# Two query units in turn in the opening, a queue of values drained later, and later C loads, in a fused attention and state-space kernel

## The chip, the cores and the metric

The kernel runs on one core of a Trainium2 chip. The metric is device time in microseconds (us) of one execution. Executions of the same kernel scatter by some us here (967.45 to 972.73 us in eleven runs of the kernel before in one call), so timed runs are given as a median or mean with their number, and a profiled execution is one execution, not the typical one. The experiments were run in three calls on three chips (runs 1 to 4, 5 to 8 and 9 to 11, in the order below), and the kernel before took 970.06, 969.35 and 969.82 us in them (means): times of different calls are compared by what they save on the kernel before of the same call.

Ratios are the mean time of one kernel's fast runs over the mean of the other's from the same rounds, so they are not quite the ratios of the medians.

Engines: TensorE (PE in the profile; PEld is its weight load), VectorE (DVE), ScalarE (ACT), GpSimd (POOL), and SyncE (SP), which issues most DMAs (257 of the 264 in the profile of before).

## The reference, cut to what matters

```python
x = A_x                                            # 1 x 2048 x 1024, bf16
g = sigmoid((x * gate_w).sum(-1, keepdims=True))
a = ssm(x, Lambda, B, C, log_dt, Dskip)            # complex diagonal scan over 2048 steps, 1024 states
qkv = x @ wqkv                                     # 32 heads of 32
p = softmax(q @ k.T * 32 ** -0.5)                  # 2048 x 2048 for each head
b = (p @ v) @ wo
return g * a + (1 - g) * b
```

The softmax has 32 x 2048 x 2048 exponentials: 1,024 instructions of 128 x 1024 on ScalarE. Everything else is arranged around them.

## The kernel before

Eight groups of four heads; in each group eight query units of 256 queries; in each unit eight *bursts* of 256 keys, one for each x block. A burst is one score instruction group on TensorE and two exponentials on ScalarE. In the main loop, one burst is one *period*. In it TensorE does the scores of burst p, the values (exponentials times V) of burst p - 2, and four "dense" 512-column matmuls of other work (projections, B, C, output); VectorE evicts a dense chain from its PSUM bank when it ends, and does the scan's arithmetic.

```python
OPENING = ("K0 B0 K1 M B1 K2 Va0 B2 Vb0 Q1 Va1 K3 Vb1 B3 Va2 Vb2 K4 Va3 B4 Vb3 K5 Va4 B5 Vb4 K6 Va5 B6 Vb5 K7 Va6 B7 "
           "Vb6 Va7 Vb7 B8 P0 P1 P2 G B9 P3 P4 P5")     # Ki: keys of x block i; Bi: burst i; Va/Vb: values; P: p @ v

def burst(self, B):
    ...
    self.S.op("pe", mm, reads=[("K", g % 2, i // 2), ("Q", qz)], writes=[("S", sl[0]), ("S", sl[1])], name="qk")
    for z in range(2):
        s, p = sl[z], self.pt_of(B, z)
        self.act(lambda e, s=s, p=p: e.activation(self.tile[p], ps[:, 2 * s:2 * s + 2, :], ACT.Exp, scale=SCALE), [("S", s)], [("pt", p)], "exp")

def build(self):
    ...
    self.ld_b(0, 0)
    self.ld_b(1, 1)                  # B's first two blocks; two buffers in all
    for part in (1, 2, 0):
        self.ld_w(1, part)
    for j in range(8):
        self.ld_c(j)                 # 16 transposing loads of C, all here
    self.opening()
    ...
    for p in range(first, NBURST):   # first = 10
        self.burst(p)
        for b in pvs.get(p, [p - 2]):
            self.pv(b)               # the values of a burst: four quarters of four matmuls
        ...                          # then four dense matmuls, then VectorE's background work
        if ended is not None:
            ended.evac()             # VectorE empties bank 7; on a chain of B's block n this also issues the load of block n + 2
```

In SyncE's timeline the DMAs go out in the order of the program, and the load of B's third block is behind the 16 C loads (33.15 to 60.61 us): it goes out at 63.99 us here.

## Time and profile before

| | before |
|---|---|
| timed, three runs | 967.69, 969.53, 971.06 us |
| the profiled execution | 974.28 us (span 972.5 us) |
| ScalarE busy | 943.8 us |
| first exponential | 9.86 us |
| half-clock windows of TensorE (granted clock 0.50) | 66.7 us (6.8 us), 865.4 us (3.4 us), 957.5 us (6.8 us), 967.8 us on |

Busy time of each engine (share of the span) and the chain of waits, from the page of before:

```profile
PE 934.1 (96%) x15308; PEld 491.0 (50%) x15308; DVE 512.8 (53%) x1096; ACT 943.8 (97%) x1034; POOL 9.4 (1%) x39
...
ACT 94%; PE 3%; DVE 1%; DMA 1%; SPq 1%; issue 0%; DVEq 0%
```

ScalarE is busy 97% of the span and carries 94% of the chain that ended last. A change can only win from its idle time. The view of ScalarE's waits has them as: who waited, for whom, us in total, times, longest.

```profile
ACT f_pt L1530 <- PE f_ps L1524: 7.6, 6, 4.5
ACT f_OT L1530 <- PE f_ps L1524: 4.8, 3, 2.3
...
ACT f_Et L1530 <- PE f_ps L1524: 1.4, 2, 0.9
```

L1524 is the score matmul and L1530 the exponential: 13.8 us of ScalarE's idle time come from scores that were late. The timeline of ScalarE (start, duration, what, count, idle time before and its releaser) shows the opening's share:

```profile
14.68 1.94 ACT L1530 ACTIVATE f_pt<-f_ps 128x1024 bf16<-128x1024 f32 x2 [0.96 <-PE f_ps L1524]
18.95 1.94 ACT L1530 ACTIVATE f_OT<-f_ps 128x1024 bf16<-128x1024 f32 x2 [2.33 <-PE f_ps L1524]
22.60 1.94 ACT L1530 ACTIVATE f_OT<-f_ps 128x1024 bf16<-128x1024 f32 x2 [1.71 <-PE f_ps L1524]
...
25.37 1.94 ACT L1530 ACTIVATE f_OT<-f_ps 128x1024 bf16<-128x1024 f32 x2 [0.74 <-PE f_ps L1524]
27.81 1.94 ACT L1530 ACTIVATE f_Et<-f_ps 128x1024 bf16<-128x1024 f32 x2 [0.50 <-PE f_ps L1524]
30.67 3.78 ACT L1530 ACTIVATE f_Et<-f_ps 128x1024 bf16<-128x1024 f32 x4 [0.92 <-PE f_ps L1524]
```

Each line is one burst of two exponentials (the last is two bursts), and before each one ScalarE idles: one x block gives it 1.83 us of work, and the blocks come more slowly (from the fourth to the ninth, 7.61 to 20.55 us, the loads are issued 2.6 us apart). The second piece is later. SyncE's timeline, around the end of the C loads (L1052), two transposes of attention output (L1569) and the load of B's third block (L1046):

```profile
59.13 1.48 SPq L1052 DMA_TRANSPOSE f_cT_im<-in_A_C_im_dram  x1
60.73 3.17 SPq L1569 DMA_TRANSPOSE f_OT<-f_On  x2
63.99 1.27 SPq L1046 DMA_TRANSPOSE f_wb<-in_A_B_re_dram  x1
```

TensorE's timeline over the same time, with the dense matmuls of B at L1414, and its recovery:

```profile
63.34 0.57 PE L1546 MATMUL f_ps<-f_V,f_pt 128*128 128x33 bf16 x16
...
67.73 1.89 PE L1414 MATMUL f_ps<-f_xT,f_wb 128*128 128x512 bf16 x4 [3.82 <-DMA f_wb<-in_A_B_re_dram]
...
73.39 1.05 PE L1414 MATMUL f_ps<-f_xT,f_wb 128*128 128x512 bf16 x4
74.38 0.40 PE L1524 MATMUL f_ps<-f_Q,f_K 32*128 32x256 bf16 x8
...
76.08 0.40 PE L1524 MATMUL f_ps<-f_Q,f_K 32*128 32x256 bf16 x8
...
77.98 0.40 PE L1524 MATMUL f_ps<-f_Q,f_K 32*128 32x256 bf16 x8
```

TensorE stands 3.82 us for B's block. The first four matmuls after it take 1.89 us, where four take 1.05 us at 73.39: the clock was halved (granted clock 0.50 from 66.7 to 73.5 us). From 74 us TensorE is behind and runs as fast as it can (busy 12.86 of 13.00 us from 74 to 87 us): its period is 1.70 us (74.38 to 76.08) when a chain goes on, and 1.90 us (76.08 to 77.98) when a new one has to wait for the bank's eviction. ScalarE's period is 1.83 us, so TensorE has little room.

**An accounting used below.** From the start times in the trace: between the 301st and the 801st exponential, ScalarE starts one every 0.9167 us. How far the n-th exponential starts behind a ScalarE that kept this pace from the first one is called its *lag*. In the profile of before it is 7.9 us at the 33rd exponential (the opening), 7.8 at the 43rd, 13.4 at the 93rd (the stall), and stays there to the 901st.

Starts have a flaw here. Where exponentials follow one another without a delay, ScalarE's records grow from 1.02 to 1.33 us (in the profile of before from the 56th to the 82nd exponential): they start every 0.904 us, while they still end every 0.917. So a lag by starts comes out up to 0.31 us lower there than a lag by ends, and seems to fall although nothing was won. Where it matters, the lag by ends is given too.

### The profile page before, as it was taken

To read this page: it belongs to the slowest core of one execution; us is meant where nothing else is said; L and a number is where in the kernel's file an instruction comes from. 1 tells how busy PE (TensorE), PEld (TensorE's weight loads), DVE (VectorE), ACT (ScalarE), POOL (GpSimd) and SP (SyncE) were. 2 spreads that over 40 slices of the span, in tenths; PEclk is the share of its full clock that TensorE was granted. 3 is DMA by queue.
4 is the path that set the end of the run, shared out by engine and by line. 5 is a ranking of instruction groups with operands and counts; after the bars stand their busy time and mean duration, and the time that the engine had idled before them with its cause. 6 is when DMAs were issued, how large, how long until landed. Compare 5 with 4: busy or idle time off the path is not lost.

```text
span 972.5 us, 33344 instructions
## 1 busy us (share of the span) xinstructions
PE 934.1 (96%) x15308; PEld 491.0 (50%) x15308; DVE 512.8 (53%) x1096; ACT 943.8 (97%) x1034; POOL 9.4 (1%) x39
## 2 busy tenths in 40 slices
PE   7989999999999999999999999999999999899996
PEld 5534644464445464554644654545544556444443
DVE  3668889889888525412268611188744112232223
ACT  4979999999999999999999999999999999999996
POOL 1000000000000000000000000000000000000000
PEclk9989999999999999999999999999999999999997
DMA  9994014311232102120023110132101213223311
GB/s 203 154 170 85 8 29 80 73 30 37 40 72 61 49 5 51 39 69 29 19 37 83 30 37 28 50 82 62 29 5 51 83 37 105 57 74 115 114 60 61
DMA packets 157074, 60.88 MB, mean 63 GB/s; under 512 B 145664, under 2 KB 145664, under 8 KB 156928
## 3 DMA queue, kind: packets, MB, share of 16 engines
q1 hardware_dynamic: 154768, 58.16, 26.9%
q8 instruction: 121, 1.98, 0.9%
q10 hardware_dynamic: 2160, 0.53, 0.3%
q14 instruction: 25, 0.20, 0.1%
HBM read 16.79 MB, written 12.58 MB: 30 GB/s over the span
## 4 chain that ended last, share of the span: by engine, by line
ACT 94%; PE 3%; DVE 1%; DMA 1%; SPq 1%; issue 0%; DVEq 0%
ACT f_pt L1530 93%; SPq L1036 1%; PE f_ps L1524 1%; ACT f_OT L1530 1%; PE f_ps L1414 1%; DMA f_xT<-in_A_x_dram 1%; PE f_ps L1546 0%; PE f_ps L1153 0%; ACT f_Et L1530 0%; DMA f_wb<-in_A_B_re_dram 0%; PE f_ps L1474 0%; DVE f_V L1158 0%; PE f_ps L1117 0%; DVE f_K L1129 0%; PE f_ps L1754 0%
## 5 line engine op out<-in xcount | busy, mean ns | idle before, releaser
L1530 ACT ACTIVATE f_pt<-f_ps 128x1024 bf16<-128x1024 f32 x1006 | 923.3, 1310 | 7.6 <-PE f_ps L1524 7.6
L1546 PEld LDWEIGHTS f_ps<-f_V,f_pt 128*128 128x128 bf16 x8048 | 234.5, 96 | 106.9 <-issue 103.5
L1546 PE MATMUL f_ps<-f_V,f_pt 128*128 128x33 bf16 x8048 | 285.6, 178 | 0.0
L1524 PE MATMUL f_ps<-f_Q,f_K 32*128 32x256 bf16 x4096 | 204.6, 274 | 24.7 <-ACT f_pt L1530 6.5
L1524 PEld LDWEIGHTS f_ps<-f_Q,f_K 32*128 32x128 bf16 x4096 | 61.0, 92 | 229.7 <-ACT f_pt L1530 222.2
L1414 PE MATMUL f_ps<-f_xT,f_wb 128*128 128x512 bf16 x512 | 132.7, 381 | 4.0 <-DMA f_wb<-in_A_B_re_dram 3.8
L1384 PE MATMUL f_ps<-f_xT,f_wb 128*128 128x512 bf16 x472 | 121.0, 378 | 0.0
L1456 DVE TENSOR_SCALAR f_Ag<-f_ps,f_gcol 128x512 f32<-128x512 f32 x32 | 24.0, 751 | 135.4 <-PE f_ps L1443 135.4
L1333 DVE TENSOR_TENSOR_SCAN f_ht<-f_pf,f_init,f_ut 128x512 bf16<-128x512 f32 x64 | 80.4, 1273 | 0.0
L1443 PE MATMUL f_ps<-f_cT_re,f_hp 128*128 128x512 bf16 x192 | 72.7, 378 | 0.0
L1443 PE MATMUL f_ps<-f_cT_im,f_hp 128*128 128x512 bf16 x192 | 72.6, 378 | 0.0
L1474 PE MATMUL f_ps<-f_wb,f_OT 128*128 128x512 bf16 x252 | 67.4, 387 | 0.1
L1480 DVE SCALAR_TENSOR_TENSOR f_xT<-f_ps,f_gcol,f_hp 128x512 bf16<-128x512 f32 (+1 forms) x28 | 21.0, 751 | 77.2 <-PE f_ps L1474 77.2
L1402 PE MATMUL f_ps<-f_wb,f_xT 128*128 128x128 bf16 x896 | 59.3, 219 | 0.0
L1414 PEld LDWEIGHTS f_ps<-f_xT,f_wb 128*128 128x128 bf16 x512 | 40.7, 96 | 36.1 <-DMA f_wb<-in_A_B_re_dram 3.9
L1420 DVE CAST f_ub<-f_ps 128x512 bf16<-128x512 f32 x48 | 33.2, 692 | 46.8 <-PE f_ps L1414 46.4
L1384 PEld LDWEIGHTS f_ps<-f_xT,f_wb 128*128 128x128 bf16 x472 | 36.9, 96 | 28.1
L1402 PEld LDWEIGHTS f_ps<-f_wb,f_xT 128*128 128x128 bf16 x896 | 50.4, 97 | 0.0
L1391 DVE CAST f_Q<-f_ps 128x512 bf16<-128x512 f32 x31 | 21.5, 692 | 54.6 <-PE f_ps L1384 54.5
L1324 DVE TENSOR_TENSOR f_tq<-f_ht,f_Et 128x512 bf16<-128x512 bf16 x128 | 45.6, 419 | 0.0
L1324 DVE TENSOR_TENSOR f_ut<-f_tq 128x512 f32<-128x512 bf16 x64 | 42.0, 685 | 0.0
L1408 DVE CAST f_V<-f_ps 128x512 bf16<-128x512 f32 x28 | 19.4, 694 | 38.2 <-PE f_ps L1402 38.0
(124 smaller groups left out, 504.2 us busy)
## 6 DMA issues: line engine op xcount, KB each, us to landing
ag_scratch<-f_Ag SPq DMA_DIRECT2D x32, 256.0 KB, 2.0
f_hp<-ag_scratch SPq DMA_DIRECT2D x32, 256.0 KB, 2.9
f_wb<-in_B_wqkv_dram SPq DMA_DIRECT2D x21, 256.0 KB, 4.5
out_dram<-f_xT SPq DMA_DIRECT2D x16, 256.0 KB, 2.1
f_wb<-in_B_wo_dram SPq DMA_DIRECT2D x1, 1024.0 KB, 5.3
f_OT<-f_On SPq DMA_TRANSPOSE x63, 2.5
f_wb<-in_B_wo_dram SPq DMA_DIRECT2D x1, 768.0 KB
f_wb<-in_B_wqkv_dram ACTq DMA_DIRECT2D x2, 256.0 KB, 4.2
```

The lines of the kernel that those rows point to most:

```text
L1324: ops.append((c, lambda: dve(lambda e: e.tensor_tensor(o, a, b, op), r, w)))
L1333: ops.append((1.29, lambda ri=ri: dve(lambda e: e.tensor_tensor_scan(ht[:, ri, :], rr, ut[:, ri, :], self.init[:, ri, j:j + 1], ALU.mult, ...
L1384: mms.append((1, lambda e, f, l, a=a: e.matmul(ps[:, bank, :], w[:, g % 2, part, a, :], xT[:, a, 512 * ch:512 * (ch + 1)], start=f, stop=l ...
L1402: m = e.matmul(ps[:, bank, 128 * q:128 * (q + 1)], xT[:, a, 128 * kt:128 * (kt + 1)], w[:, g % 2, 2, a, :], start=(a == 0), stop=(a == 7))
L1414: mms.append((1, lambda e, f, l, a=a: e.matmul(ps[:, 7, :], bT[:, n % 2, ri, a, :], xT[:, a, 512 * ch:512 * (ch + 1)], start=f, stop=l), [ ...
L1420: self.dve(lambda e: e.tensor_copy(self.ub[k][:, ri, :], ps[:, 7, :]), [("bank", 7)], [("ub", k, ri)] + over, "evac_u")
L1443: mms.append((1, lambda e, f, l, j=j, ri=ri: e.matmul(ps[:, 7, :], hp[:, ri, j, cols], cT[ri][:, j, 512 * cb:512 * (cb + 1)], start=f, sto ...
L1456: self.dve(lambda e: e.tensor_scalar(a, ps[:, 7, :], self.gcol[:, 0, tt:tt + 1], None, ALU.mult), [("bank", 7), "g0"], [at], "evac_c")
L1474: mms.append((1, lambda e, f, l, j=j: e.matmul(ps[:, 7, :], OT[:, j, 256 * qb + 128 * r:256 * qb + 128 * (r + 1)], wo[j][0][:, 512 * cb:51 ...
L1524: m = e.matmul(ps[:, 2 * sl[h // 2] + h % 2, 256 * kl:256 * (kl + 1)], K[32 * h:32 * h + 32, g % 2, 128 * kt:128 * (kt + 1)], Q[32 * h:32 ...
L1530: self.act(lambda e, s=s, p=p: e.activation(self.tile[p], ps[:, 2 * s:2 * s + 2, :], ACT.Exp, scale=SCALE), [("S", s)], [("pt", p)], "exp")
L1546: m = e.matmul(ps[:, 6, o:o + 33], self.tile[p][:, h2, 256 * kl + 128 * qt:256 * kl + 128 * (qt + 1)], V[:, g % 2, 2 * i + kl, h, :], star ...
```

## The change

The intent: keep ScalarE fed while x lands, by taking two query units for each x block; let the exponentials of those 16 bursts wait in a queue of tiles, since no value matmuls are done in the opening; drain the queue with one or two quarters more in each period; and load C later, into space that the queue used first, so that B's loads are not behind it. The diff, cut to its core:

```diff
+FIRST = 16
+RING = 60
+C_LOADS = 28
...
-        pte = four(self.Et[:].rearrange("p r j t -> p (r j t)")[:, 0:6144])
-        self.tile = [self.pt[:, t] for t in range(6)] + [ptx[:, t] for t in range(6)] + [pte[:, t] for t in range(6)]
+        pte = four(self.Et[:].rearrange("p r j t -> p (r j t)"))
+        self.tile = [self.pt[:, t] for t in range(6)] + [ptx[:, t] for t in range(6)] + [pte[:, t] for t in range(8)]
+        self.tile += [self.cT[ri][:, j, :].rearrange("p (h n) -> p h n", h=2) for j in range(8) for ri in range(2)]
...
-    OPENING = ("K0 B0 K1 M B1 K2 Va0 B2 Vb0 Q1 Va1 K3 Vb1 B3 Va2 Vb2 K4 Va3 B4 Vb3 K5 Va4 B5 Vb4 K6 Va5 B6 Vb5 K7 Va6 B7 "
-               "Vb6 Va7 Vb7 B8 P0 P1 P2 G B9 P3 P4 P5")
+    OPENING = ("K0 B0.0 Ka1 Kb1 M B0.1 Qa1 Qb1 Va0 B1.0 Ka2 Kb2 B1.1 Vb0 Ka3 B0.2 Kb3 Va1 Ka4 B0.3 Kb4 Vb1 B0.4 Ka5 Kb5 B1.2 Va2 Ka6 "
+               "B0.5 Kb6 Vb2 Ka7 B0.6 Kb7 Va3 B0.7 Vb3 Qa2 Qb2 B1.3 Va4 Vb4 B1.4 Qa3 Qb3 Va5 B1.5 Vb5 B1.6 Va6 Vb6 B1.7 Va7 Vb7 G")
...
+        for p in range(FIRST, NBURST + 1):
+            n = min(4 * (p - 1), done + (12 if p < FIRST + 0 else 5), done // 32 * 32 + 32)
+            left = done // 32 * 32 + 32 - done
+            if 5 < left < 13 and 4 * (p - 1) >= done + 6:
+                n = done + 6
+            self.quarters[p] = (done, n)
... (each queued burst gets one of 18 pairs of tiles, for as long as its values are waited for)
-        for j in range(8):
-            self.ld_c(j)
+        self.plan()
         self.opening()
...
-        pvs = {10: [6, 7], 11: [8], 12: [9, 10]}
         for p in range(first, NBURST):
...
-            for b in pvs.get(p, [p - 2]):
-                self.pv(b)
+            q0, q1 = self.quarters[p]
+            self.pv(q0, q1)
...
+            if p >= C_LOADS and p % 4 == 0 and nc < 8:
+                self.ld_c(nc)
+                nc += 1
```

In `B1.2` the first number is the query unit, the second the x block; `Ka3` and `Kb3` are the halves of a key projection.

More of the change, by code (lines that the diff above doesn't have):

```diff
@@ L1052, in ld_c @@
             self.dma(lambda e, ri=ri, src=src: e.dma_start_transpose(self.cT[ri][:, j, :], src[:, 128 * j:128 * (j + 1)]),
-                     [], [("cT", ri, j)], "ld_cT")
+                     [], [("cT", ri, j), ("pt", 20 + 2 * j + ri)], "ld_cT")
     def begin(self):
@@ L1109, in piece, with half256 @@
             yield lambda mm=mm, kw=kw, r=r: self.S.op("pe", mm, reads=[("w", 0, part), ("xr", r)], name="proj", **kw)
-    def pieces256(self, part, i, bank):
+    def half256(self, part, i, half):
         ps, w, xT = self.ps, self.w, self.xT
@@ L1115, in mm @@
             m = None
-            for a in range(8):
-                m = e.matmul(ps[:, bank, 0:256], w[:, 0, part, a, :], xT[:, a, 256 * i:256 * (i + 1)], start=(a == 0), stop=(a == 7))
+            for a in range(4 * half, 4 * half + 4):
+                m = e.matmul(ps[:, 7, 0:256], w[:, 0, part, a, :], xT[:, a, 256 * i:256 * (i + 1)], start=(a == 0), stop=(a == 7))
             return m
-        self.S.op("pe", mm, reads=[("w", 0, part), ("xr", 2 * i), ("xr", 2 * i + 1)], writes=[("bank", bank)], name="proj")
+        self.S.op("pe", mm, reads=[("w", 0, part), ("xr", 2 * i), ("xr", 2 * i + 1)], name="proj", **(dict(acc=[("bank", 7)]) if half else dict(writes=[("bank", 7)])))
     def opening(self):
@@ L1132, in opening @@
         for word in self.OPENING.split():
-            op, i = word.rstrip("0123456789"), word.lstrip("KQVabPBMG")
-            i = int(i) if i else 0
+            op = word.rstrip("0123456789.")
+            i = word[len(op):]
+            U, i = [int(v) for v in i.split(".")] if "." in i else (0, int(i or 0))
             if op == "K":
-                if i == 0:
-                    for a, b in zip(self.piece(1, 0, 7, True), self.piece(0, 0, 6, True)):
-                        a()
-                        b()
-                    evac(self.Q[:, 0, 0:256], 6, ("Q", 0), True, self.act)
-                else:
-                    self.pieces256(1, i, 7)
+                for a, b in zip(self.piece(1, 0, 7, True), self.piece(0, 0, 6, True)):
+                    a()
+                    b()
+                evac(self.Q[:, 0, 0:256], 6, ("Q", 0), True, self.act)
+                evac(self.K[:, 0, 0:256], 7, ("K", 0, 0), True)
+            elif op in ("Ka", "Qa"):
+                self.half256(int(op == "Ka"), i, 0)
+            elif op == "Kb":
+                self.half256(1, i, 1)
                 evac(self.K[:, 0, 256 * i:256 * (i + 1)], 7, ("K", 0, i // 2), i % 2 == 0)
-            elif op == "Q":
-                self.pieces256(0, i, 7)
-                evac(self.Q[:, 0, 256 * i:256 * (i + 1)], 7, ("Q", 0), False)
+            elif op == "Qb":
+                self.half256(0, i, 1)
+                evac(self.Q[:, i // 2, 256 * (i % 2):256 * (i % 2 + 1)], 7, ("Q", i // 2), i % 2 == 0)
+                self.spare(0.5)
             elif op in ("Va", "Vb"):
-                bank, h, kt = 7 if i == 7 else 6, int(op == "Vb"), 2 * i + int(op == "Vb")
+                bank, h, kt = 6, int(op == "Vb"), 2 * i + int(op == "Vb")
                 def mm(e, kt=kt, h=h, bank=bank):
@@ L1160, in opening @@
                     dve(lambda e, i=i, src=src: e.tensor_copy(self.gcol[:, 0, 2 * i:2 * i + 2], src[:, :, 128]), [("bank", bank)], [("g0", i)])
-                    self.spare(0.9)
+                    self.spare(1.0)
             elif op == "G":
@@ L1167, in opening @@
                 dve(lambda e: e.tensor_scalar(g[:, 1, :], g[:, 0, :], -1.0, 1.0, ALU.mult, ALU.add), ["g0"], ["g1"])
-            elif op == "P":
-                if i == 0:
-                    S.tok_w["O"] = S.tok_w[("bank", 6)]
-                    S.tok_r["O"] = list(S.tok_r[("bank", 6)])
-                self.pv(i)
             elif op == "B":
-                self.p = i
-                self.burst(i)
-                while self.later and self.later[0][0] <= i:
+                self.burst(8 * U + i)
+                while self.later and self.later[0][0] <= self.p:
                     self.later.pop(0)[1]()
+                self.p += 1
             elif op == "M":
@@ L1300, in table_ops @@
         first = ["m_a0", "m_a1", "m_a2", "m_k", "m_h", "m_y", "m_s"] if j == 0 else []
-        over = [("pt", 12 + t) for t in range(6)] if j == 0 else []
+        over = [("pt", 12 + j // 2), ("pt", 16 + j // 2)]
         ops = []
@@ L1506, in st_out, with plan @@
                  [("fin", fb, 0), ("fin", fb, 1)], [("outd", tt)], "st_out")
+    def plan(self):
+        self.quarters, done = {}, 0
+        used = {}
+        for p in range(FIRST, NBURST + 1):
[4 more added lines that the diff above has]
+            self.quarters[p] = (done, n)
+            for q in range(done, n):
+                used[q // 4] = p
+            done = n
+        order = [8 * int(w[1]) + int(w[3]) for w in self.OPENING.split() if w[0] == "B"]
+        assert sorted(order) == list(range(FIRST))
+        when = {b: p for p, b in enumerate(order)}
+        pairs = [((12 + t, 16 + t), FIRST + 4 + 14 * t) for t in range(4)] + [((10, 11), FIRST + 6)]
+        pairs += [((20 + 2 * j, 21 + 2 * j), C_LOADS + 4 * j) for j in range(8)] + [((6, 7), 68), ((8, 9), 68)]
+        pairs += [((2 * r, 2 * r + 1), NBURST) for r in range(3)]
+        free = {t: -9 for t, _ in pairs}
+        self.pt_at = {}
+        for b in sorted(range(RING), key=lambda b: when.get(b, b)):
+            p = when.get(b, b)
+            ok = [(end, t) for t, end in pairs if free[t] < p and used[b] < end and not (end == NBURST and used[b] >= RING + t[0] // 2)]
+            assert ok, (b, p)
+            near = [(end, t) for end, t in ok if end - used[b] <= 1]
+            end, t = min(near) if near else max(ok)
+            free[t] = used[b]
+            self.pt_at[b] = t
     def pt_of(self, B, z):
-        return 2 * B + z if B < 9 else 2 * B - 18 + z if 12 <= B < 15 else (2 * B + z) % 6
+        return self.pt_at[B][z] if B < RING else (2 * B + z) % 6
     def burst(self, B):
@@ L1515, in burst @@
         ps, K, Q = self.ps, self.K, self.Q
-        sl = [(2 * B) % 3, (2 * B + 1) % 3]
+        sl = [(2 * self.p) % 3, (2 * self.p + 1) % 3]
         qz, qo = (4 * g + qb // 2) % 5, 256 * (qb % 2)
@@ L1530, in burst, with pv, mm @@
             self.act(lambda e, s=s, p=p: e.activation(self.tile[p], ps[:, 2 * s:2 * s + 2, :], ACT.Exp, scale=SCALE), [("S", s)], [("pt", p)], "exp")
-    def pv(self, B, zs=(0, 1)):
-        U, i = divmod(B, BURSTS)
-        g, qb = divmod(U, QUNITS)
+    def pv(self, q0, q1):
         ps, V = self.ps, self.V
-        for z in zs:
+        for q in range(q0, q1):
+            B, z, kl = q // 4, q // 2 % 2, q % 2
+            U, i = divmod(B, BURSTS)
+            g = U // QUNITS
             p = self.pt_of(B, z)
-            def mm(e, z=z, p=p):
+            def mm(e, z=z, p=p, kl=kl, i=i, g=g):
                 m = None
-                for kl in range(2):
-                    for h2 in range(2):
-                        for qt in range(2):
-                            h = 2 * z + h2
-                            o = 33 * (4 * qt + h)
-                            m = e.matmul(ps[:, 6, o:o + 33], self.tile[p][:, h2, 256 * kl + 128 * qt:256 * kl + 128 * (qt + 1)], V[:, g % 2, 2 * i + kl, h, :],
-                                         start=(i == 0 and z == 0 and kl == 0 and h2 == 0 and qt == 0), stop=(i == BURSTS - 1 and kl == 1),
-                                         skip_group_check=True)
+                for h2 in range(2):
+                    for qt in range(2):
+                        h = 2 * z + h2
+                        o = 33 * (4 * qt + h)
+                        m = e.matmul(ps[:, 6, o:o + 33], self.tile[p][:, h2, 256 * kl + 128 * qt:256 * kl + 128 * (qt + 1)], V[:, g % 2, 2 * i + kl, h, :],
+                                     start=(i == 0 and z == 0 and kl == 0 and h2 == 0 and qt == 0), stop=(i == BURSTS - 1 and kl == 1),
+                                     skip_group_check=True)
                 return m
-            kw = dict(writes=["O"]) if i == 0 and z == 0 else dict(acc=["O"])
+            kw = dict(writes=["O"]) if i == 0 and z == 0 and kl == 0 else dict(acc=["O"])
             self.S.op("pe", mm, reads=[("pt", p), ("V", g % 2, i // 2), "v1"], name="pv", **kw)
@@ L1585, in build @@
             self.ld_w(1, part)
-        for j in range(8):
-            self.ld_c(j)
+        self.plan()
         self.opening()
+        S.tok_w["O"] = S.tok_w[("bank", 6)]
+        S.tok_r["O"] = list(S.tok_r[("bank", 6)])
         for j in range(8):
             self.bg2 += self.table_ops(j)
-        for cb in range(2):
-            for j in range(8):
-                self.bg2 += self.fold_ops(j, cb)
-        start = [self.d_qk(0, 0, 1)]
         proj = {g: [self.d_qk(g, 1, c) for c in range(4)] + [self.d_v(g, f) for f in range(4)] + [self.d_qk(g, 0, c) for c in range(4)]
@@ L1622, in build @@
         cur = None
-        first = 10
+        first = FIRST
         wo1 = last = False
-        nal = 0
+        nal = nc = 0
         self.c_end = 0
         log = self.log = []
-        pvs = {10: [6, 7], 11: [8], 12: [9, 10]}
         for p in range(first, NBURST):
             g, pg = divmod(p, 64)
-            assert not proj[g] or g == 0
+            assert not proj[g] or (g == 0 and p < 32)
+            self.p = p
             self.burst(p)
@@ L1634, in build @@
             period = PERIOD
-            for b in pvs.get(p, [p - 2]):
-                self.pv(b)
-                if b % BURSTS == BURSTS - 1:
-                    self.normalize(b // BURSTS)
-                    self.dve_t = max(self.dve_t, t0 + PE_HEAD) + 0.75
-            self.p = p
+            q0, q1 = self.quarters[p]
+            self.pv(q0, q1)
+            if q1 % 32 == 0:
+                self.normalize(q1 // 32 - 1)
+                self.dve_t = max(self.dve_t, t0 + PE_HEAD) + 0.75
+            if p >= C_LOADS and p % 4 == 0 and nc < 8:
+                self.ld_c(nc)
+                nc += 1
+                if nc == 8:
+                    for cb in range(2):
+                        for j in range(8):
+                            self.bg2 += self.fold_ops(j, cb)
             while self.later and self.later[0][0] <= p:
@@ L1644, in build @@
             if pg == 24 and g + 2 < GROUPS:
-                assert g or not proj[0]
+                assert g or not (proj[0] or cur and cur.tag == "proj")
                 for part in (1, 2, 0):
@@ L1663, in build @@
             used = 0.0
-            quota = 2 if p in (10, 12) else MM_PER_PERIOD
+            quota = MM_PER_PERIOD if p >= FIRST + 0 else 0
             ended = None
@@ L1669, in build @@
                         break
-                    if start:
-                        cur = start.pop(0)
-                    elif p == first + 1:
-                        break
+                    if proj[0] and p >= FIRST + 4:
+                        cur = proj[0].pop(0)
                     elif not last:
-                        if g == 0 and proj[0]:
-                            cur = proj[0].pop(0)
-                        else:
-                            nxt = proj[g + 1]
-                            left = 64 - pg
-                            need = 2 * len(nxt)
-                            u_ok = c_ok = False
-                            if us:
-                                ch, n, ri, dn = us[0]
-                                hp_free = ch < 2 or (ch == 2 and self.c_left[0] == 0) or (ch == 3 and self.c_left[2] == 0)
-                                u_ok = ri == 1 or (self.items_done >= n - (3 if n < 18 else 1) and hp_free)
-                            if cs:
-                                c_ok = self.items_done >= 8 * (cs[0][0] + 1) and p > self.item_p + 1 and len(self.folded) >= cs[0][2]
-                            n_ok = nxt and pg >= nxt[0].after
-                            if n_ok and left <= need + 4:
-                                cur = nxt.pop(0)
-                            elif c_ok and cs[0][0] == 1 and p + 4 * sum(self.c_left[:2]) + need >= 254:
-                                cur = cs.pop(0)[1]
-                            elif u_ok:
-                                cur = us.pop(0)[3]
-                            elif c_ok:
-                                cur = cs.pop(0)[1]
-                            elif n_ok:
-                                cur = nxt.pop(0)
@@ new lines, in build @@
+                        nxt = proj[g + 1]
+                        left = 64 - pg
+                        need = 2 * len(nxt)
+                        u_ok = c_ok = False
+                        if us:
+                            ch, n, ri, dn = us[0]
+                            hp_free = ch < 2 or (ch == 2 and self.c_left[0] == 0) or (ch == 3 and self.c_left[2] == 0)
+                            u_ok = ri == 1 or (self.items_done >= n - (3 if n < 18 else 1) and hp_free)
+                        if cs:
+                            c_ok = self.items_done >= 8 * (cs[0][0] + 1) and p > self.item_p + 1 and len(self.folded) >= cs[0][2]
@@ new lines, in build @@
+                        n_ok = nxt and pg >= nxt[0].after
+                        if n_ok and left <= need + 4:
+                            cur = nxt.pop(0)
+                        elif c_ok and cs[0][0] == 1 and p + 4 * sum(self.c_left[:2]) + need >= 254:
+                            cur = cs.pop(0)[1]
+                        elif u_ok:
+                            cur = us.pop(0)[3]
+                        elif c_ok:
+                            cur = cs.pop(0)[1]
+                        elif n_ok:
+                            cur = nxt.pop(0)
@@ L1756, in tail @@
         check(0, 63, 0, 63, 0)
-        self.pv(NBURST - 2)
+        self.pv(4 * NBURST - 8, 4 * NBURST - 4)
         preload()
-        self.pv(NBURST - 1)
+        self.pv(4 * NBURST - 4, 4 * NBURST)
         ov = ps[:, 6, 0:264].rearrange("p (a c) -> p a c", a=8)
```

## The prediction

> **What bounds it now.** ScalarE's 1,024 exponentials (128x1024 each). The page's first part has ScalarE busy 943.8 of 972.5 us, the chain of waits runs 94% through it, and the timeline spaces two exponentials 1.835 us apart. Only ScalarE's idle 28.7 us can be won; its waits and timeline place it:
> - before the first exponential at 9.86 us: about 7.9 us;
> - the opening, to 31 us: 7.2 us in six gaps (0.96, 2.33, 1.71, 0.74, 0.50, 0.92), each before a score matmul that waits for the next x block's projection. x loads are issued 2.6 us apart; a burst of one query unit is 1.83 us of exponentials;
> - 65.7 to 73 us: 4.51 + 0.89 = 5.4 us. TensorE stood 3.8 us for B's third block, issued only at 63.99 us because SyncE was issuing 16 C transposes (33.2 to 60.7 us). TensorE then ran at half rate (four 128x512 matmuls in 1.89 us, not 1.02). [...]
> - about 8 us of tail, 0.6 us near 865 us.
>
> **What the change does.** Two query units per x block give 3.67 us of exponentials against 2.6 us of arrival, so the six gaps should close. C loads start at burst 28, two per four bursts, behind B's loads: the 5.4 us stall goes. The work is the same in number; three 256-column query projections move into the opening.
>
> **What it costs.** Values start at burst 16, some 60 quarters behind, and catch up with 5 or 6 quarters per burst over 42 bursts (from the plan: 28 of 5, 14 of 6). A quarter is four value matmuls at 26 ns, 0.105 us. TensorE has little room: where it catches up after the stall (73 to 87 us), its own period is 1.70 us, and 1.90 us when a chain ends and bank 7 waits for VectorE's 0.69 us eviction. With 5 quarters these become 1.81 and 1.90 us (the extra hides in the eviction wait), with 6 both 1.91. Chains end every second burst, so I estimate a mean of 1.87 against ScalarE's 1.835: 0.037 x 42 = 1.5 us, less some 0.25 us of slack in the score buffers: +1.3 us. All of it is on the critical path. Remaining opening gaps: estimate 0.7 us.
>
> **Prediction.** 969.5 - 7.2 + 0.7 - 5.4 + 1.3 = 958.9 us, say 959; range 955.5 to 963.5. The 2% mark, 950.1 us, would need 19 us, more than gaps and stall together: faster 0.03, same 0.95, slower 0.02.
>
> **What would show each step.** (1) Between 9.9 and 39.5 us ScalarE idles about 1 us, not 7; the 33rd exponential starts near 39.5 instead of 47.1 us. (2) No wait of TensorE on B's load, no half clock between 60 and 80 us; C transposes spread from about 61 to 115 us. (3) Between 39 and 117 us ScalarE idles in many small gaps before score matmuls, about 1.3 us in sum; before has none there besides the stall. (4) ScalarE busy within 1 us of 943.8; about 9 us of tail after the last exponential, as before.
>
> **What would make it wrong.** TensorE more strained in the catch-up (VectorE late with evictions because table building waits for queued tiles): several us more. A later x block reopening gaps in the opening. A C load that waits for its tile's values blocks SyncE, and B's load behind it: a stall of some us comes back. On the other side, TensorE may absorb the drain entirely: 957.5.

The 0.25 us of slack in the score buffers is an estimate that no run measured.

## The result, and the profile after

Four timed runs: median 961.67 us (960.9 to 962.08), against 969.14 us of before (967.69 to 971.06, four runs). The ratio is 0.9921, 95% interval 0.9902 to 0.994. Two more calls gave 0.9913 and 0.9918 for the same pair. This is inside the predicted range and inside 2%.

The profiled executions differ by more than the timed ones: spans of 972.5 and 960.1 us, 12.3 us apart, where the medians are 7.5 us apart. So the profile of before shows something that the usual execution has less of; the first experiment looks at this.

The page of after, the same two lines:

```profile
PE 928.0 (97%) x15316; PEld 490.1 (51%) x15316; DVE 513.2 (53%) x1097; ACT 944.0 (98%) x1034; POOL 10.1 (1%) x39
...
ACT 96%; SPq 1%; PE 1%; DVE 1%; DMA 1%; issue 0%; DVEq 0%
```

ScalarE's busy time is the same within 0.2 us. Its waits for scores are two short ones, 13.8 us become 1.2 (the change's edits move L1524 and L1530 to L1559 and L1565 in the kernel after):

```profile
ACT f_pt L1565 <- PE f_ps L1559: 0.6, 1, 0.6
ACT f_Et L1565 <- PE f_ps L1559: 0.6, 1, 0.6
```

ScalarE's timeline in the opening has one gap left, of 0.58 us:

```profile
15.30 3.78 ACT L1565 ACTIVATE f_OT<-f_ps 128x1024 bf16<-128x1024 f32 x4
...
19.75 3.77 ACT L1565 ACTIVATE f_Et<-f_ps 128x1024 bf16<-128x1024 f32 x4 [0.58 <-PE f_ps L1559]
23.39 1.06 ACT L1565 ACTIVATE f_cT_re<-f_ps 128x1024 bf16<-128x1024 f32 x1
```

SyncE issues B's third block (L1050) at 42.99 us, as soon as its buffer is free, and the C loads (L1056) from 65.86 us on:

```profile
42.99 1.24 SPq L1050 DMA_TRANSPOSE f_wb<-in_A_B_re_dram  x1
...
65.86 1.30 SPq L1056 DMA_TRANSPOSE f_cT_re<-in_A_C_re_dram  x1
67.20 2.20 SPq L1056 DMA_TRANSPOSE f_cT_im<-in_A_C_im_dram  x1
```

The lag is 0.8 us at the 33rd exponential and 2.0 us at the 93rd. So 7.1 us came from the opening; in this pair of profiles 5.5 us more came from the stall, and 1.2 us were lost in the catch-up, between the two marks. (The queue is empty only at the 116th exponential, after the second mark; by the ends of the records, and to that point, the loss is 1.30 us.) That loss can hardly be seen as idle time. Busy time of the engines from 60 to 80 us and from 80 to 117 us (window, its length, then PE, PEld, DVE, ACT and POOL busy, TensorE's granted clock, DMA share and GB/s), before first:

```profile
60.00:80.00 20.00, 16.07 (x218) 6.92 (x214) 11.97 (x26) 14.60 (x17) 0.00 (x0) 0.83 0.82 151
80.00:117.00 37.00, 36.17 (x651) 20.75 (x648) 32.22 (x64) 37.00 (x42) 0.00 (x0) 1.00 0.17 36
```

And after:

```profile
60.00:80.00 20.00, 20.00 (x363) 10.73 (x363) 16.88 (x34) 20.00 (x22) 0.00 (x0) 1.00 0.79 129
80.00:117.00 37.00, 37.00 (x769) 24.14 (x767) 31.17 (x64) 37.00 (x41) 0.00 (x0) 1.00 0.63 99
```

After, *both* engines are busy 100% from 60 to 117 us, and one of them must be the slower. The starts of the score matmuls (L1559) in TensorE's timeline tell which. Between them are value matmuls and four dense ones; the first two lines are the end of the first chain and its successor's start, further up at 43 us:

```profile
42.92 0.40 PE L1559 MATMUL f_ps<-f_Q,f_K 32*128 32x256 bf16 x8
...
44.30 1.02 PE L1416 MATMUL f_ps<-f_xT,f_wb 128*128 128x512 bf16 x4 [0.37 <-DVE f_pf L1211]
...
56.39 0.40 PE L1559 MATMUL f_ps<-f_Q,f_K 32*128 32x256 bf16 x8
...
58.20 0.40 PE L1559 MATMUL f_ps<-f_Q,f_K 32*128 32x256 bf16 x8
...
60.10 0.40 PE L1559 MATMUL f_ps<-f_Q,f_K 32*128 32x256 bf16 x8
...
62.01 0.40 PE L1559 MATMUL f_ps<-f_Q,f_K 32*128 32x256 bf16 x8
```

The periods are 1.81, 1.90 and 1.91 us, as the prediction had worked them out from the recovery of before (1.81 with five quarters, 1.90 to 1.91 else), against ScalarE's 1.83. The 26 ns of a value matmul, on which the estimates rest, are in the traces: 16 of 33 columns take 0.41 us from their first start to that of the next group (73.55 to 73.96 us in the profile of after).

The first two lines, at 42.92 and 44.30 us, show another loss: a chain could not start at once because of VectorE. VectorE's timeline has the eviction (L1422) at 43.46 us, queued behind background arithmetic, although the chain's last matmul had ended about 42.96 us:

```profile
43.19 0.36 DVE L1252 TENSOR_SCALAR f_OT<-f_OT 128x384 f32<-128x384 f32 x1
43.46 0.68 DVE L1422 CAST f_ub<-f_ps 128x512 bf16<-128x512 f32 x1
```

### The profile page after: what moved, and what is told of

Same layout as the page of the kernel before. It is cut to its first block, busy times and chain, and to the rows that moved or that the text cites. A ratio compares the mean times of both kernels' runs of the same rounds, so it can differ in the third digit from the quotient of the medians.

```text
span 960.1 us, 33364 instructions
## 1 busy us (share of the span) xinstructions
PE 928.0 (97%) x15316; PEld 490.1 (51%) x15316; DVE 513.2 (53%) x1097; ACT 944.0 (98%) x1034; POOL 10.1 (1%) x39
## 4 chain that ended last, share of the span: by engine, by line
ACT 96%; SPq 1%; PE 1%; DVE 1%; DMA 1%; issue 0%; DVEq 0%
ACT f_pt L1565 89%; ACT f_OT L1565 2%; ACT f_Et L1565 2%; ACT f_cT_re L1565 2%; ACT f_cT_im L1565 2%; SPq L1040 1%; DMA f_xT<-in_A_x_dram 1%; PE f_ps L1559 0%; PE f_ps L1789 0%; PE f_ps L1582 0%; PE f_ps L1161 0%; PE f_ps L1416 0%; DVE f_xT L1828 0%; PE f_ps L1121 0%; PE f_ps L1815 0%
## 5 line engine op out<-in xcount | busy, mean ns | idle before, releaser
L1565 ACT ACTIVATE f_pt<-f_ps 128x1024 bf16<-128x1024 f32 x944 | 867.1, 1309 | 0.6 <-PE f_ps L1559 0.6
L1582 PEld LDWEIGHTS f_ps<-f_V,f_pt 128*128 128x128 bf16 x7552 | 220.2, 96 | 99.2 <-issue 98.8
L1582 PE MATMUL f_ps<-f_V,f_pt 128*128 128x33 bf16 x7552 | 268.7, 178 | 0.0
L1559 PE MATMUL f_ps<-f_Q,f_K 32*128 32x256 bf16 x4096 | 203.3, 273 | 22.7 <-ACT f_pt L1565 4.4
L1559 PEld LDWEIGHTS f_ps<-f_Q,f_K 32*128 32x128 bf16 x4096 | 60.5, 92 | 224.2 <-ACT f_pt L1565 205.8
L1416 PE MATMUL f_ps<-f_xT,f_wb 128*128 128x512 bf16 x512 | 131.0, 377 | 0.5 <-DVE f_pf L1211 0.4
L1386 PE MATMUL f_ps<-f_xT,f_wb 128*128 128x512 bf16 x464 | 118.9, 378 | 0.0
L1595 DVE RECIPROCAL f_rc<-f_ps 128x8 f32<-128x8 f32 x63 | 13.1, 208 | 107.3 <-PE f_ps L1582 107.1
L1422 DVE CAST f_ub<-f_ps 128x512 bf16<-128x512 f32 x48 | 33.2, 691 | 39.7 <-PE f_ps L1416 39.7
```

What stands on the lines that cost most here:

```text
L1386: mms.append((1, lambda e, f, l, a=a: e.matmul(ps[:, bank, :], w[:, g % 2, part, a, :], xT[:, a, 512 * ch:512 * (ch + 1)], start=f, stop=l ...
L1416: mms.append((1, lambda e, f, l, a=a: e.matmul(ps[:, 7, :], bT[:, n % 2, ri, a, :], xT[:, a, 512 * ch:512 * (ch + 1)], start=f, stop=l), [ ...
L1422: self.dve(lambda e: e.tensor_copy(self.ub[k][:, ri, :], ps[:, 7, :]), [("bank", 7)], [("ub", k, ri)] + over, "evac_u")
L1559: m = e.matmul(ps[:, 2 * sl[h // 2] + h % 2, 256 * kl:256 * (kl + 1)], K[32 * h:32 * h + 32, g % 2, 128 * kt:128 * (kt + 1)], Q[32 * h:32 ...
L1582: m = e.matmul(ps[:, 6, o:o + 33], self.tile[p][:, h2, 256 * kl + 128 * qt:256 * kl + 128 * (qt + 1)], V[:, g % 2, 2 * i + kl, h, :], star ...
```

## The experiments

All kernels gave correct outputs. The lags in us, worked out from the start times of the exponentials in each run's trace, with the tail (from the start of the last exponential to the end). The last column is the loss by the ends of the records, from the 33rd exponential to the 201st, when the queue has long been empty:

| run | 33rd | 43rd | 93rd | 301st | 1024th | tail | loss by ends, 33rd to 201st |
|---|---|---|---|---|---|---|---|
| before | 7.89 | 7.77 | 13.37 | 13.37 | 14.48 | 10.36 | 5.61 |
| before again | 8.09 | 7.96 | 11.49 | 11.49 | 11.71 | 10.62 | 3.62 |
| C spaced alone | 7.75 | 7.63 | 7.61 | 7.62 | 7.84 | 10.42 | 0.00 |
| after | 0.78 | 1.23 | 1.99 | 1.99 | 2.17 | 10.51 | 1.30 |
| after, same | 0.36 | 0.80 | 1.55 | 1.56 | 1.60 | 10.76 | 1.29 |
| after, anchor | 0.63 | 1.07 | 1.82 | 1.82 | 1.82 | 9.88 | 1.29 |
| sixes at chain starts | 0.93 | 1.38 | 1.73 | 1.71 | 1.71 | 9.70 | 0.86 |
| sixes where none starts | 0.79 | 1.20 | 2.15 | 2.23 | 2.24 | 9.53 | 1.59 |
| score before x4 | 0.10 | 0.53 | 1.28 | 1.28 | 1.29 | 9.83 | 1.28 |
| C bunched | 0.97 | 1.42 | 2.17 | 3.21 | 3.21 | 9.81 | 2.31 |
| three edits | 0.32 | 0.33 | 0.67 | 0.65 | 0.87 | 9.90 | 0.44 |
| three edits, again | 0.81 | 0.76 | 1.10 | 1.08 | 1.08 | 10.36 | 0.43 |
| filled tail | 0.62 | 0.57 | 0.91 | 0.89 | 0.89 | 9.88 | 0.42 |

The theory is the prediction's: three terms (opening, stall, catch-up), the first two won, the last paid. Its rivals are named with each run.

### The kernel before, profiled again

No edit.

> The kernel before, unchanged, for a second profile. The accounting used here: how far the n-th exponential starts behind a ScalarE that starts one every 0.9167 us from the first. In the first profile of before it is 7.9 us behind at the 33rd and 13.4 us behind at the 93rd, and the clock was halved for 6.8 us at 66.7 us; yet that execution was 974.3 us where the timed ones are 967.7 to 971.1. Theory A (the stall costs 5.5 us in every execution): about 7.9 and 13.4 us again, half clock near 67 us again. Theory B (the wait for B's third block is in every execution, but the half clock and part of the stall's length are a matter of luck): again 7.9 us at the 33rd, but only 9 to 11.5 us at the 93rd, with no or less half clock near 67 us.

Measured: one execution of 971.55 us. The opening lags 8.1 us, the 93rd exponential 11.5 us. The wait for B's block is there again, but the block was issued at 60.92 us, not at 63.99, TensorE stood 2.66 us, not 3.82, and the clock was halved for 3.4 us, not 6.8. SyncE's timeline has the load:

```profile
60.92 1.26 SPq L1046 DMA_TRANSPOSE f_wb<-in_A_B_re_dram  x1
```

TensorE's timeline has the wait, and four matmuls after it at full speed still:

```profile
66.48 1.06 PE L1414 MATMUL f_ps<-f_xT,f_wb 128*128 128x512 bf16 x4 [2.66 <-DMA f_wb<-in_A_B_re_dram]
```

The busy times from 60 to 80 us have a mean clock of 0.91, where the first profile has 0.83:

```profile
60.00:80.00 20.00, 17.14 (x251) 7.75 (x247) 13.95 (x27) 16.59 (x19) 0.00 (x0) 0.91 0.91 140
```

The stall cost 3.5 us here and 5.6 us in the first profile (lag at the 93rd less lag at the 43rd). Its size is a matter of the execution: theory B. The block's own transfer is part of it: from issue to landing it took 5.51 us here and 3.69 us in the first profile, so of the 3.07 us by which it was issued earlier only 1.16 reached TensorE. The halved stretches are 3.41 us long here and 6.83 us in the first profile, and begin at 67.4 and 66.7 us. The half-clock window near 865 us of the first profile, 0.9 us of lag, is not there either.

### C spaced, and nothing else

```diff
-        for j in range(8):
-            self.ld_c(j)
         self.opening()
...
+            if p >= 28 and p % 4 == 0 and nc < 8:
+                self.ld_c(nc)
+                nc += 1
```

> The kernel before with one part of the change alone: C loads spaced, two per four bursts from burst 28, opening as before. Both theories: no wait of TensorE on B's third block in the profile, ScalarE 7.9 us behind at the 33rd exponential and the same 7.9 at the 93rd. Theory A: 5.5 us faster in the timed runs, near 963.6 us, ratio near 0.9943. Theory B: 1 to 2.5 us faster, 966.6 to 968.1 us, ratio 0.9975 to 0.999.

(The edit also puts the folding of C, background work of VectorE, behind the last C load, as the kernel after does.)

Measured: mean 967.26 us (966.80 to 967.99, six runs) against 970.06 us of before (967.45 to 972.73, eleven runs); ratio 0.997, interval 0.9955 to 0.9986. That is 2.8 us: half of theory A's 5.5, a little more than theory B allowed; the interval, 1.4 to 4.4 us, excludes theory A but not theory B. The lag stays at 7.6 us from the 43rd to the 901st exponential, SyncE issues B's third block at 51.69 us, and the stall and its slow clock are gone (SyncE's timeline, then the busy times):

```profile
51.69 1.23 SPq L1046 DMA_TRANSPOSE f_wb<-in_A_B_re_dram  x1
```

```profile
60.00:80.00 20.00, 19.68 (x309) 9.37 (x308) 16.99 (x36) 20.00 (x23) 0.00 (x0) 1.00 0.86 153
```

The spread of the runs fell as well, from 5.3 us to 1.2 us. The fastest of the eleven runs of before is as fast as this kernel: in such an execution the stall probably cost almost nothing. None of those was profiled, but its mean clock, 0.997 against 0.989 to 0.996 of the other ten, says that it had the least half-clock time.

### The kernel after, on the same chip

No edit.

> The kernel after, unchanged, as the anchor for variants on the same chip. Both theories: 961 to 962 us, ratio near 0.992; in its profile 0.8 us behind at the 33rd exponential and 2.0 us at the 93rd, as in its first profile.

Measured: 961.64 us in the mean (960.99 to 962.39, five runs), ratio 0.9913; the lags are 0.36 and 1.55 us, 0.4 us less than expected, as the gap at the fifth x block is shorter (0.15 us). Against the kernel with C spaced alone, 5.6 us are won by the rest of the change: 7.4 us of opening less 1.2 us of catch-up is 6.2 us in the two profiles, less 0.3 us by which the tail is longer. From the 33rd to the 93rd exponential this run, the first profile and a third one (below) lose 1.19, 1.21 and 1.19 us, and always 0.44 to 0.45 of it before the 43rd.

### The six-quarter bursts at chain starts

```diff
-            if 5 < left < 13 and 4 * (p - 1) >= done + 6:
+            if (p - FIRST) % 6 in (2, 4) and p < FIRST + 42:
                 n = done + 6
```

> The kernel after, but the two bursts of a unit that drain six quarters are always ones in which a chain of dense matmuls starts (third and fifth of each unit, in place of fifth and sixth), where the extra value matmuls hide in the wait for the bank's eviction. Same work, same number of bursts. Theory (TensorE's own period is over ScalarE's in the catch-up): seven quarters of 0.105 us no longer stick out, so the 1.2 us lost between the 33rd and the 93rd exponential fall to about 0.5 us, and the time falls by 0.7 us against the unchanged kernel after. Rival (VectorE late with evictions or table building is what costs there): the loss stays at 1.2 us within 0.2.

Measured: the loss from the 43rd to the 93rd exponential fell from 0.75 to 0.35 us; the 0.45 us before the 43rd stayed. So the total fell to 0.80 (0.86 by the ends, from 1.29), not to 0.5 us: both the theory and the rival are part of it. TensorE's starts in the same place show five quarters where no chain starts (1.80 to 1.81 us) and six hidden where one does (1.90):

```profile
56.54 0.40 PE L1559 MATMUL f_ps<-f_Q,f_K 32*128 32x256 bf16 x8
...
58.34 0.40 PE L1559 MATMUL f_ps<-f_Q,f_K 32*128 32x256 bf16 x8
...
60.24 0.40 PE L1559 MATMUL f_ps<-f_Q,f_K 32*128 32x256 bf16 x8
...
62.05 0.40 PE L1559 MATMUL f_ps<-f_Q,f_K 32*128 32x256 bf16 x8
```

The time fell to 960.54 us (mean of four), 1.1 us under the kernel after. Only 0.4 us of that is the catch-up; in the profiles the rest is the tail, 9.70 us against 10.76, where this run had one half-clock window less.

### The six-quarter bursts where no chain starts

```diff
-            if 5 < left < 13 and 4 * (p - 1) >= done + 6:
+            if (p - FIRST) % 6 in (1, 3) and p < FIRST + 42:
                 n = done + 6
```

> The opposite of the run with sixes at chain starts: both six-quarter bursts of a unit (second and fourth) are ones in which no chain starts, so no eviction wait hides the extra value matmuls. Same work. Theory (TensorE's period is over ScalarE's in the catch-up): the loss between the 43rd and the 93rd exponential, 0.75 us in the kernel after and 0.35 us with sixes at chain starts, rises to 1.1 to 1.5 us, and the time to 0.3 to 0.7 us above the kernel after (962 to 962.5 us). Rival (placement of the quarters does not matter, the gain of the other placement was chance or the tail's clock): 0.75 us within 0.15.

Measured: 0.95 us from the 43rd to the 93rd, in place of 0.75, and 0.35 with the opposite placement. The order is the theory's, the size under the 1.1 to 1.5 us it asked for, and just over the rival's 0.90. By the ends of the records and to the end of the drain, the loss after the 43rd is 1.33 us, against 1.07 in the kernel after and 0.63 with the opposite placement. The time, 961.28 us (mean of five), can't show so little: this call had no kernel after, and what it saves on the kernel before, 8.1 us against 8.4, is within the scatter. Placement matters, by 0.6 to 0.7 us of lag from end to end.

### Scores before the x block that is late

```diff
-... Kb3 Va1 Ka4 B0.3 Kb4 Vb1 B0.4 ...
+... Kb3 Va1 B0.3 Ka4 Kb4 Vb1 B0.4 ...
```

> The kernel after, with one word of the opening moved: the scores of the fourth block's burst go before, not after, the first half of the fifth block's key projection, which waits for the x load. Theory (the one gap left in the opening, 0.15 to 0.74 us near 19.3 us, is TensorE standing in order at a projection whose x block has not landed): the gap goes, ScalarE is 0.2 to 0.35 us behind at the 33rd exponential instead of 0.4 to 0.9, and the time falls by 0.3 to 0.5 us, to near 961.2 us. Rival (the gap only moves to the next burst, because the key block is then late for it): behind by 0.4 to 0.9 us as now.

Measured: in this run's profile the gap is gone, the lag at the 33rd is 0.10 us. The time is 961.39 us in the mean (five runs): 8.0 us saved on the kernel before of this call, where the kernel after saved 8.4 us in its own. No gain is seen in it. The same edit is in the three runs with all edits, and there the lag at the 33rd is 0.32, 0.81 and 0.62 us. In the run of the filled tail, for one, TensorE stands for the next x block instead:

```profile
21.18 1.05 PE L1121 MATMUL f_ps<-f_xT,f_wb 128*128 128x256 bf16 x8 [0.49 <-DMA f_xT<-in_A_x_dram]
```

So the rival is right in some executions: the gap moves to the next block. What is left of the opening follows when x lands, and that the edit doesn't change. Whether it is worth a few tenths is not settled.

### C loads in one go, later

```diff
-            if p >= C_LOADS and p % 4 == 0 and nc < 8:
+            while p >= C_LOADS + 28 and nc < 8:
```

> The kernel after, but all 16 C transposes are issued in one go at burst 56 (near 113 us), not two per four bursts from burst 28. Theory (it is SyncE's in-order issue of transposes, some 1.5 us each, that delays B's blocks, not how early C is loaded): SyncE is held about 25 us, one of B's blocks is issued late, TensorE stands 3 to 8 us for it near 140 us, ScalarE loses 3 to 9 us there, and the time is 3 to 9 us above the kernel after. Rival (the stall of the kernel before came from x, weights and C competing for the transfer engines in the opening): no stall, within 0.7 us of the kernel after.

Measured: SyncE issued C from 108.1 to 133.1 us without pause, B's block after it, and TensorE stood for it, but for 1.30 us and not for 3 to 8. (In the first profile of the kernel after the same load goes out at 125.02 us.) SyncE's timeline, with its last C load and B's load:

```profile
131.87 1.24 SPq L1056 DMA_TRANSPOSE f_cT_im<-in_A_C_im_dram  x1
...
134.49 2.10 SPq L1050 DMA_TRANSPOSE f_wb<-in_A_B_re_dram  x1
```

TensorE's timeline, with the wait:

```profile
138.26 1.04 PE L1416 MATMUL f_ps<-f_xT,f_wb 128*128 128x512 bf16 x4 [1.30 <-DMA f_wb<-in_A_B_re_dram]
```

The lag grows by 1.0 us between the 93rd and the 301st, where the kernel after has none. The time, 961.84 us (mean of four), saves 7.5 us on the kernel before of this call, where the kernel after saved 8.4 us in its own: it agrees with a loss of 1.0 us, but does not show it by itself. The stall's mechanism is shown at another place and time, away from x: 25 us of C loads in SyncE's stream hold B's block back. Its size was over-estimated: TensorE came to the block at 136.96 us (138.26 less 1.30), 2.5 us after its load had been issued, and the clock was not halved after it: the four matmuls that had waited took 1.04 us, the next four (at 139.98 us) 1.02.

### Three edits together

Sixes at chain starts, the score order of above, and VectorE's planned time started 1.0 us later, so that less background work is put before the first eviction:

```diff
         first = FIRST
+        self.dve_t = 1.0
```

> A version meant to beat both: sixes at chain starts, the fourth block's scores before the fifth block's projection, and VectorE's planned time started 1.0 us later, so that the first chain's eviction near 43.5 us is not queued behind background work. Theory: the three terms add, ScalarE 0.2 to 0.4 us behind at the 33rd exponential, no step of 0.45 us at the 38th, 0.35 us from the 43rd to the 93rd; about 0.7 to 1 us at the end; time 959.3 to 960.2 us. Rival (the eviction's lateness is not from the background work): the step at the 38th stays, 960 to 960.6 us.

Measured: the step before the 43rd is gone (0.32 to 0.33 us), and the loss to the 93rd is 0.34 us. The chain's last matmul ends at 42.52 us, and VectorE's timeline has the eviction at 42.56:

```profile
42.56 0.69 DVE L1422 CAST f_ub<-f_ps 128x512 bf16<-128x512 f32 x1 [0.31 <-PE f_ps L1416]
```

TensorE's next chain then starts without a wait:

```profile
43.43 1.02 PE L1416 MATMUL f_ps<-f_xT,f_wb 128*128 128x512 bf16 x4
```

The median is 960.08 us, in the expected range, but two of five runs were 961.46 and 962.67 us, and the ratio to before, 0.9913, is that of the kernel after in its own call.

### Again, with the kernel after and a filled tail on the same chip

The filled tail has the three edits and:

```diff
+            if p >= NBURST - 4:    # six matmuls of 248 columns, onto columns of the value bank that nobody reads
+                    for k in range(6):
+                        m = e.matmul(self.ps[:, 6, 264:512], self.ident[:], self.diagD[:].rearrange("p j n -> p (j n)")[:, 0:248], start=False, stop=False, ...)
```

> The kernel after again, as the anchor on the same chip for the next two. Both theories: 961.3 to 962 us.

> The version with all three edits again, because its five times of the last call lay between 959.97 and 962.67 us. Theory (it saves 0.9 us of ScalarE's idle time in the catch-up, and the scatter comes from half-clock windows near the end, which fall differently in each execution): 960.0 to 961 us in the median, 0.7 to 1.4 us under the anchor. Rival (the saving is within the scatter): within 0.5 us of the anchor.

> All three edits, and in the last four bursts, in which TensorE has one dense matmul instead of four, six matmuls of 248 columns more each, that add to columns of the value bank nobody reads; outputs stay correct. Theory (TensorE's clock is halved in the last 12 us [...], and the tail's matmuls then run at half rate): no half-clock window before the last exponential, the tail after it 0.5 to 1.2 us shorter than the 9.5 to 10.8 us of the other runs, time 0.5 to 1.2 us under the version with three edits, 959 to 960 us. Rival (the windows start in the tail itself, where TensorE waits for VectorE): tail unchanged within 0.3 us.

Measured: the kernel after 961.71 us (mean of five), three edits 960.29 us (mean of four, 959.82 to 960.67), filled tail 959.94 us (mean of four, 959.78 to 960.18); ratios to before 0.9918, 0.9901 and 0.9898. The three edits save 1.4 us here, and all four times lie under all five of the kernel after; the call before had no kernel after to compare with. Of the lag they save 0.7 us (1.82 to 1.08 at the last exponential); the rest these two profiles don't account for, as their tails differ the other way (9.88 and 10.36 us). The filled tail is not clear of them by time: 0.35 us. In its profile the clock stayed at full speed until after the last exponential, as was expected. Busy times of 3.41 us, as long as the shortest half-clock window, in the last four bursts, first in the kernel after (the run "on the same chip" above, whose clock was halved next, at 947.8 us: four 512-column matmuls took 1.87 us at 949.35), then with the filled tail (clock at full speed to 956.3 us):

```profile
944.39:947.80 3.41, 1.99 (x50) 1.10 (x48) 1.50 (x2) 3.41 (x5) 0.00 (x0) 1.00 0.21 79
```

```profile
942.65:946.06 3.41, 3.33 (x63) 2.19 (x62) 1.50 (x2) 3.41 (x5) 0.00 (x0) 1.00 0.21 77
```

TensorE is busy 1.99 us of the one window and 3.33 of the other. That the filling kept the clock up is not shown, though: five profiles without it (sixes at chain starts, sixes where none starts, score before x4, C bunched, and the kernel after as anchor) have no half-clock window before the last exponential either. Their tails are 9.53 to 9.88 us, and the filled one's is 9.88; the seven profiles that have such a window, before and after alike, have tails of 9.90 to 10.76 us. So a clock that is halved before the last exponential goes with a tail that is longer by 0.65 us in the mean, and the same kernel has it in one execution and not in another (the kernel after: 10.51, 10.76 and 9.88 us). How much of that the filling saves, one profile can't tell. The filled tail has the lowest mean time measured, 1.8 us under the kernel after in the same call.

## Why the prediction was right or wrong

It was right in the sum, 959 predicted and 961.7 measured, inside the range. Point by point:

- **What bounds the kernel.** Right: ScalarE's busy time is 943.8 and 944.0 us, and all of the gain is idle time of ScalarE.
- **"The six gaps should close"**, 7.2 us less 0.7 left. Right: the lag at the 33rd exponential fell from 7.9 (8.1, 7.75 in other runs) to 0.78 (0.36, 0.63). The 0.7 left was meant for the start of the second unit and the last x block; in truth most of it is one gap at the fifth x block, which lands late by a time that differs in each execution.
- **"The 5.4 us stall goes."** It goes, but this term of the sum was mis-sized. The prediction read 5.4 us from one execution and took it off a median of others. The same record said that this execution took 974.3 us while the timed ones took 967.7 to 971.1, and this should have warned me. A second profile has 3.5 us, and undoing the stall alone gave 2.8 us in timed runs. Three things differ between the two profiles: when SyncE gets through the C loads (B's block issued at 60.9 or 64.0 us), how long the block's own transfer takes (5.5 or 3.7 us), and how many half-clock windows follow (3.4 or 6.8 us).
- **"+1.3 us" of catch-up.** Right in size: 1.19 to 1.21 us by the starts from the 33rd to the 93rd, and 1.29 to 1.30 us by the ends to the end of the drain, in three profiles. (By starts the lag then falls by 0.3 us, in the first profile of after from 2.3 at the 121st to 2.0 at the 201st; by the ends it stays at 2.30, so no slack comes back.) Right in mechanism for 1.07 us by the ends: the periods of 1.81, 1.90 and 1.91 us are those estimated, and moving the six-quarter bursts moves this loss to 0.63 or 1.33. The other 0.23 us, 0.45 by the starts, is one late eviction of VectorE, which the prediction had only among its risks; starting VectorE's plan later removed it (0.00 by the ends in the three runs that have it). So the sum fits to the tenth partly by luck. Why the worst placement costs only 0.26 us more, where 0.35 to 0.75 was expected, stays open.
- **"ScalarE idles in many small gaps"**, as the sign of the catch-up. Wrong as a sign: the views show ScalarE 100% busy there. Records of consecutive exponentials overlap, 1.02 us long or more and 0.92 apart, so one that is up to 0.1 us late leaves no idle time. Only their times show it, the ends better than the starts.
- **The rest.** Before 970.06 us, less 2.8 for the stall, 7.1 for the opening, plus 1.3 of catch-up: 961.5 us, where 961.6 was measured. That is closer than the tails of single executions agree, so some of it is luck.

## What to carry to other kernels

When one engine sets the pace, give it two units of work for each block of input that lands, and let the work that follows queue up; the price is a catch-up on another engine, and it can be estimated from a stretch in which that engine already runs behind. Before a stall read in a profile is taken off a median, compare the profiled execution's own time with the timed ones, and profile again if they differ. And when an engine is 100% busy, compare the ends of its instructions with their best spacing: small delays hide where the records overlap (here 1.02 us long or more, and 0.92 apart), and starts move when the records change their length.
